# Key parts moved out a unit sooner, half of the sums split around the scores, slots and gates of one batch in one set of products

## The chip, the cores and the metric

The kernel runs on one core of a Trainium2 chip. A core has five engines that run side by side, each through its own instructions in order: TensorE (PE in the profile; PEld are its weight loads), VectorE (DVE), ScalarE (ACT), GpSimd (POOL) and SyncE (SP, which issues most DMAs here). They wait for one another through semaphores. The metric is the time of one execution in microseconds (us); lower is better.

## What is computed

Three stages in a row, float32 at the interface except for the weights of the second:

```python
# 1. bucketed attention: B=2, H=8, S=768, D=64, 6 projection bits
q_bucket = bits((q @ proj) > 0); k_bucket = bits((k @ proj) > 0)
scores = where(q_bucket == k_bucket, q @ k.T / 8, -1e9)
attn = softmax(scores)
x = (attn @ v) reshaped to 1536 x 512
# 2. gated layer, d_ff = 1536
y = ((x @ w_a) * (x @ w_b)) @ w_out
# 3. eight experts, d_ff = 1024: each token goes to the expert whose embedding is nearest
expert = argmax(cosine(y, emb) / tau); gate = softmax(...)[expert]
out[token] = gate * (relu(y @ w1[expert]) @ w2[expert])
```

The weights of stage 2 arrive as 64-bit floats and are converted on the chip; products that need more precision than one pass gives are made from a high and a low part of each operand.

## The kernel before

**Order.** The program runs under a manual schedule: what the Python code issues first on an engine runs first on that engine. Two places write that order out.

**Attention** (`attention`, lines 62 to 358) runs over 48 units `u` of 256 queries each: a pair of heads `i` has six units (`r = u % 6`), a head three (`s = u % 3`). A unit has two tiles `t`. For each, TensorE makes scores (`scores`, L205 and L208) in one of two PSUM tiles `st`; VectorE takes the row maximum (`rowmax`, L213); ScalarE the exponential with its sum (`expo`, L219), which frees the PSUM tile; GpSimd normalizes (`normal`, L228 to L232); two units later VectorE transposes the tile (`turn`, L239); and TensorE multiplies by the values (`pv`, L248, "the sums"), 24 blocks a head, in two PSUM tiles `pvb` of two banks each. The sums of a head run 12 blocks at the end of a unit with `s = 0` and 12 at the end of the next. In the unit with `s = 2` ScalarE copies the sums out (`epilogue`, L268), first one `pvb` tile, then the other.

The same two `pvb` tiles then serve the preparation of a later pair. Which one depends on the unit: the last unit of a pair transposes the keys and queries of a pair to come (`turned`, L114, L128), the third makes the sign bits of the next pair (`signs`, L154 to L181). Keys use `pvb[1]`, queries `pvb[0]`. The key part is issued on TensorE as soon as the first `epilogue` has freed its tile (`fresh`), the query part at the end of the unit. Each returns a function that moves the result out of PSUM. These functions are held in `preps` and called in the next unit, after its first exponential. The key signs go to a tile `sk` and to the list `later`; `masks()` (L143), called in each unit right ahead of `preps`, makes the two masked copies `kf` from `sk`.

Other work hangs on hooks in the units: `plan` lists, for conversions of the first weights (`split64`: the steps rest, top, low, add, size, guard, parts on VectorE, GpSimd and ScalarE), the unit of each of the seven steps.

**The rest** is a list `main` of named steps, with `after` and `chain` hanging side jobs behind them: `chain` puts one job behind each following step. `("p", c, t, f, w, h)` is half a product of the gated layer (six matmuls), `("o", c, t, m)` an output product, `("h", ...)`, `("t", ...)`, `("e", ...)` are hidden rows, their transposes and output products of the first expert. The routing of each of the two batches `b` runs between these: `route_choose` finds the expert (VectorE, L712 to L726), `route_places` each token's place (TensorE L734, L740; VectorE L747 to L755, which ends in six selection tiles `sel`), `route_slots` multiplies `sel` with token numbers (L771) to get the list of tokens that `gather` fetches, `route_gates` makes the gates (VectorE L789 to L799 with an exponential on ScalarE between), `route_gate_slots` multiplies the same `sel` with the gates (L806). `transpose_in` (L851) turns gathered rows. All of them draw on two PSUM tiles of the tag `rt` in turn.

Of the kernel before, what the change touches and what calls it, by code (L numbers as in the profile page):

```python
# [9 lines left out]
F32R = mybir.dt.float32r  # L10
# [15 lines left out]
class Kernel:  # L26
# [37 lines left out]
    def attention(self, xh, xl, pools, hook):  # L64
        nc = self.nc
# [249 lines left out]
        for u in range(NU + 2):  # L315
# [10 lines left out]
            if act:  # L326
                rowmax(u, 0)
                scores(u, 1)
            moves = [((u - 8) // 3, g) for g in (1, 0)] if s == 2 and u >= 8 else []
            for m in moves[:2 if u == NU - 1 else 1]:  # L330
# [27 lines left out]
            if new < len(pairs):  # L358
                preps, held, held_kind = fresh + [kind(new, x) for x in (1, 0)[len(fresh):]], new, kind
            elif s < 2 and u >= 6:  # L360
                pv((u - 6) // 3, range(12 * s, 12 * s + 12))
            hook(u, 0)
# [52 lines left out]
class Experts:  # L415
# [312 lines left out]
    def route_places(self, b):  # L728
# [20 lines left out]

        tl = self.tl = self.small("tl", [128, TB, 2, E], F32R)  # L750
        nc.vector.tensor_tensor(tl[:, :, 0], f32(oh), self.wide(self.tok), ALU.mult)
# [14 lines left out]
    def route_slots(self, b):  # L766
        nc = self.nc
        TB, E = self.TB, self.E
        q = self.rt.tile([128, 512], F32, tag="rt", name="slots")
        for t in range(TB):  # L770
            nc.tensor.matmul(  # L771
                q[:, :2 * E], self.sel[b, t], self.tl[:, t].rearrange("p a e -> p (a e)"),
                start=(t == 0), stop=(t == TB - 1),
            )
        gi = self.gi[b] = self.small("gi", [128, E], I32)
        nc.vector.tensor_copy(gi, q[:, :E])

        big = 4096.0
        oi = self.small("oif", [128, E])
        nc.vector.tensor_scalar(oi, q[:, E:2 * E], -big, big + b * self.S, ALU.mult, ALU.add)  # L780
        nc.vector.tensor_tensor(oi, oi, q[:, :E], ALU.add)
        so = self.so[b] = self.small("so", [128, E], I32)
        nc.vector.tensor_copy(so, oi)

    def route_gates(self, b):
# [10 lines left out]
        nc.vector.tensor_tensor(tg, f32(self.oh[b]), self.wide(gt), ALU.mult)  # L796
        th = self.th = self.small("th", [128, TB, 2, E], F32R)
        nc.vector.tensor_copy(th[:, :, 0], tg)
        nc.vector.tensor_tensor(th[:, :, 1], tg, f32(th[:, :, 0]), ALU.subtract)  # L799

    def route_gate_slots(self, b):
# [3 lines left out]
        for t in range(TB):  # L805
            nc.tensor.matmul(  # L806
                q[:, :2 * E], self.sel.pop((b, t)), self.th[:, t].rearrange("p a e -> p (a e)"),
                start=(t == 0), stop=(t == TB - 1),
            )
        sg = self.sg[b] = self.small("sg", [128, E])  # L810
        nc.vector.tensor_copy(sg, q[:, :E])
# [231 lines left out]
def tile_kernel(ctx, tc, q, k, v, proj, w_a, w_b, w_out, emb, tau, w1, w2, out, dbg=None):  # L1043
# [5 lines left out]
    with tc.manual_schedule():  # L1049
# [15 lines left out]
        with tc.tile_pool(name="conv", bufs=1, side="left") as X.conv, \  # L1065
# [7 lines left out]
            def late():  # L1073
# [8 lines left out]
                (3, 4, 5, 6, 6, 9, 12), (7, 10, 11, 12, 12, 13, 18), (15, 17, 19, 22, 22, 23, 28), (21, 25, 26, 28, 28, 29, 34),  # L1082
                (42, 43, 43, 44, 44, 44, 45),
            )
# [130 lines left out]
        after(("o", L, 2, 2), split, 0, 6, G)  # L1215
        after(("o", L, 3, 2), split, 0, 7, G)
        after(("e", 0, 1, 0), X.transpose_in, 1, 0)
        after(("e", 0, 1, 1), X.transpose_in, 1, 1)
# [10 lines left out]
        def begin():  # L1229
# [9 lines left out]
            (T, 3), (T, 4), [(T, 5), (X.route_norm, 0)], (GL, 1), [(GT, 1), (X.route_choose, 0)],  # L1239
            None, None, None, (X.route_places, 0), None, [(X.route_slots, 0), (X.gather, 0, 0)],  # L1240
            (X.route_gates, 0), None, None, None, None, None, (X.route_gate_slots, 0),
        ])
        chain(("o", L, 2, 1), [(T, 6), (T, 7), (T, 8), (GL, 2), (GT, 2)])
        after(("p", L, 3, 1, 1, 1), begin)
        after(("o", L, 3, 0), X.transpose_in, 0, 0)
        after(("o", L, 3, 0), X.gather, 1, 0)
# [7 lines left out]
        after(("e", 0, 0, 2), X.gather, 1, 1)  # L1254
        after(("e", 0, 1, 0), X.route_gate_slots, 1)
        after(("h", 1, 0), X.route_most)
# [46 lines left out]
```

## Time and profile before

| | |
|---|---|
| median of 3 runs | 738.56 us (737.71 to 740.46) |
| the profiled execution | 737.05 us, of which the profile spans 735.3 us |
| TensorE busy over the span | 702.2 us (96%) |
| VectorE, GpSimd, ScalarE busy | 463.3, 440.6, 353.4 us |
| granted TensorE clock, mean | 0.997 |

The profile shows one execution. Busy time is the time in which an engine had an instruction running; "idle before" a row is the time its engine stood before it, with what ended the wait. Neighbours on one engine overlap a little, so a row's length and the distance to the next row's start differ.

### The profile page before, as it was taken

The numbers are of one execution on the slowest core, as the hardware profiler recorded it, in microseconds if no ns is written. First come the engines' busy times: TensorE is split into PE (matmuls) and PEld (weight loads), VectorE is DVE, ScalarE is ACT, GpSimd is POOL, SyncE is SP. The second block draws the span as 40 slices with busy tenths as digits, with TensorE's granted clock in tenths as the row PEclk, the third lists the DMA queues.
The fourth block names the chain that finished last, engine by engine and source line by source line (L and its number), as shares of the span: only waits on it lengthen the run. The fifth ranks groups of instructions, "written<-read, shape, count | busy, mean of one in ns | idle before, by whom it ended". The sixth has DMA issues, their size and how long they took to land.

```text
span 735.3 us, 16440 instructions
## 1 busy us (share of the span) xinstructions
PE 702.2 (96%) x6793; PEld 582.2 (79%) x6793; DVE 463.3 (63%) x675; ACT 353.4 (48%) x651; POOL 440.6 (60%) x453
## 2 busy tenths in 40 slices
PE   6799998999989999999999999999999999999996
PEld 4355554555658999999999999998888999889995
DVE  3999989888885554645646546534744865555650
ACT  4677877787664333212121212234436655556551
POOL 1777998988785572653645636634513866556651
PEclk9999999999999999999999999999999999999998
DMA  6955567364233230220211211354251966566510
GB/s 160 182 127 138 115 144 162 84 130 118 46 90 119 81 116 1 91 83 23 93 58 58 63 53 58 121 162 148 70 175 33 297 240 204 212 223 244 204 56 23
DMA packets 68605, 88.31 MB, mean 120 GB/s; under 512 B 28963, under 2 KB 41123, under 8 KB 68528
## 3 DMA queue, kind: packets, MB, share of 16 engines
q1 hardware_dynamic: 64320, 79.49, 37.5%
q0 software_dynamic: 2560, 7.34, 2.6%
q8 instruction: 54, 0.88, 0.5%
q10 hardware_dynamic: 1648, 0.39, 0.3%
q14 instruction: 23, 0.19, 0.1%
HBM read 75.52 MB, written 7.34 MB: 113 GB/s over the span
## 4 chain that ended last, share of the span: by engine, by line
PE 78%; DVE 7%; ACT 4%; issue 4%; DMA 4%; POOL 2%; SPq 1%; POOLq 0%; DVEq 0%; ACTq 0%
PE ab L548 24%; PE yp L580 13%; PE op L924 10%; PE hp L874 10%; PE pv L248 8%; PE st L205 5%; DVE nm L213 3%; ACT e L219 2%; DVE et L239 2%; PE part L548 2%; PE hr L892 2%; DMA vr<-in_v_dram 1%; PE xgt L851 1%; PE st L208 1%; DMA raw<-in_k_dram 1%
## 5 line engine op out<-in xcount | busy, mean ns | idle before, releaser
L548 PE MATMUL ab<-xh,w 128*128 128x384 f32 x704 | 185.7, 338 | 0.0
L548 PEld LDWEIGHTS ab<-xh,w 128*128 128x128 f32 x704 | 127.7, 188 | 2.0 <-issue 1.2
L548 PE MATMUL ab<-xl,w 128*128 128x384 f32 x352 | 118.3, 336 | 0.0
L563 POOL TENSOR_TENSOR g<-a,g 128x384 fp32r<-128x384 f32 x48 | 53.9, 1123 | 106.1 <-ACT g L562 106.1
L830 POOL TENSOR_TENSOR w<-raw,w 128x1024 fp32r<-128x1024 f32 x36 | 88.1, 2448 | 35.7 <-ACT w L829 34.6
L219 ACT ACTIVATE e<-st,nm 128x768 f32<-128x768 f32 x96 | 86.6, 903 | 41.1 <-DVE nm L213 19.9
L580 PE MATMUL yp<-w,g 128*128 128x512 f32 x432 | 102.9, 390 | 0.0
L213 DVE TENSOR_REDUCE nm<-st 128x1 f32<-128x768 f32 x96 | 90.2, 940 | 19.3 <-PE st L208 19.0
L232 POOL TENSOR_SCALAR e<-e,s,mc 128x768 f32<-128x768 f32 x96 | 95.2, 999 | 5.4 <-POOL s L230 0.2
L239 DVE STREAM_TRANSPOSE et<-e 128x768 f32<-128x768 f32 x96 | 92.3, 963 | 3.3 <-issue 1.3
L205 PE MATMUL st<-ks,qs 64*128 64x384 f32 x192 | 85.6, 526 | 8.9 <-ACT e L219 8.2
L205 PE MATMUL st<-k,q 64*128 64x384 f32 x192 | 85.8, 527 | 8.0 <-ACT e L219 7.0
L580 PEld LDWEIGHTS yp<-w,g 128*128 128x128 f32 x432 | 80.4, 188 | 14.9
L924 PE MATMUL op<-w,hth 128*128 128x512 f32 x256 | 80.8, 396 | 0.0
L874 PE MATMUL hp<-xgh,w 128*128 128x256 f32 x448 | 80.7, 281 | 0.0
L562 ACT CAST g<-a 128x384 fp32r<-128x384 f32 x48 | 24.7, 515 | 105.1 <-DVE a L561 105.1
L248 PEld LDWEIGHTS pv<-et,vr 32*64 32x64 f32 x3072 | 59.6, 130 | 19.3 <-issue 9.3
L248 PE MATMUL pv<-et,vr 32*64 32x192 f32 x3072 | 71.1, 325 | 3.8 <-ACT q L128 1.9
L830 DVE TENSOR_TENSOR w<-raw,w 128x1024 fp32r<-128x1024 f32 x28 | 64.9, 2316 | 14.4 <-ACT w L829 14.2
L874 PEld LDWEIGHTS hp<-xgh,w 128*128 128x128 f32 x448 | 69.1, 188 | 0.3
L548 PEld LDWEIGHTS ab<-xl,w 128*128 128x128 f32 x352 | 66.2, 188 | 0.8
L557 ACT COPY a<-ab 128x384 f32<-128x384 f32 x44 | 21.0, 478 | 94.6 <-PE ab L548 93.2
(202 smaller groups left out, 1242.2 us busy)
## 6 DMA issues: line engine op xcount, KB each, us to landing
raw<-in_moe_w_dram SPq DMA_DIRECT2D x32, 1024.0 KB, 5.2
vr<-in_v_dram SPq DMA_DIRECT2D x64, 192.0 KB, 4.2
raw<-in_moe_w_a_dram SPq DMA_DIRECT2D x5, 1024.0 KB, 5.2
raw<-in_moe_w_b_dram SPq DMA_DIRECT2D x5, 1024.0 KB, 5.1
raw<-in_moe_w_out_dram SPq DMA_DIRECT2D x5, 1024.0 KB, 5.0
raw<-in_k_dram SPq DMA_DIRECT2D x16, 192.0 KB, 4.9
qs<-q SPq DMA_DIRECT2D x16, 192.0 KB, 4.0
ybuf<-y SPq DMA_DIRECT2D x12, 256.0 KB, 6.0
```

What stands on the lines that cost most here:

```text
L205: nc.tensor.matmul(st[:, n, :H2], q[d, ql], k[d], start=True, stop=False, tile_position=(64 * n, 0))
L213: nc.vector.tensor_reduce(NM[u][:, t:t + 1], ST[u, t][:, :, :H2], axis=AX.XY, op=ALU.max, negate=True)
L219: nc.scalar.activation(e, ST.pop((u, t))[:, :, :H2], AF.Exp, bias=NM[u][:, t:t + 1], accum_out=SU[u][:, t:t + 1])
L232: nc.gpsimd.tensor_scalar(E[u, t], E[u, t], r[:, t:t + 1], c[:, t:t + 1], ALU.mult, ALU.add)
L239: nc.vector.transpose(ET[h][:, :, c], E.pop((u, t)).rearrange("p a (b s) -> p (a b) s", s=32))
L248: nc.tensor.matmul(pvb[a // 2][m:m + 64, a % 2, :NC * 32], v[d], et[d, n].rearrange("p c s -> p (c s)"), start=(n < 2), stop=(n >= NB32 - ...
L548: nc.tensor.matmul(p[:, :384], w[:, k, fs], x[:, k, cols], start=(k == 0 and n == 0), stop=(k == self.KD - 1 and n == 2),)
L563: nc.gpsimd.tensor_tensor(gl[:, f], a, f32(gh[:, f]), ALU.subtract)
L580: nc.tensor.matmul(p, g[:, f, rows], w[:, f], start=(n == 0), stop=(n == 5))
L830: eng.tensor_tensor(l, raw, f32(h), ALU.subtract)
L874: nc.tensor.matmul(p[:, :256], w[:, k, fs], x[:, k], start=(n == 0), stop=(n == 3 * self.KD - 1))
L924: nc.tensor.matmul(p, h[:, 2 * n + f, rows], w[:, f], start=(n == 0 and f == 0 and m == 0), stop=(n == 3 and f == 1 and m == 2),)
```

## The change

The function that moves a key part out is called in the unit that issued it, after that unit's second exponential; the query part stays held for the next unit. Of the first twelve blocks of a head's sums, six stay at the end of the unit with `s = 0`, and six go into the next unit between its two scores. In the plan of the first weights' last piece, `guard` and `parts` move one unit later. For the first batch, gates are computed before places, and slots and gates come from one set of products with 32 columns; its places, slots and transpose move one step later in the list. For the second batch, the gate products come before the transpose that follows the same step.

```diff
@@ -326,6 +326,8 @@
             if act:
                 rowmax(u, 0)
                 scores(u, 1)
+            if s == 1 and u >= 7:
+                pv((u - 7) // 3, range(6, 12))
             moves = [((u - 8) // 3, g) for g in (1, 0)] if s == 2 and u >= 8 else []
             for m in moves[:2 if u == NU - 1 else 1]:
                 epilogue(*m)
@@ -356,9 +358,11 @@
             if act:
                 expo(u, 1)
             if new < len(pairs):
-                preps, held, held_kind = fresh + [kind(new, x) for x in (1, 0)[len(fresh):]], new, kind
+                for prep in fresh:
+                    prep(nc.scalar)
+                preps, held, held_kind = [kind(new, x) for x in (1, 0)[len(fresh):]], new, kind
             elif s < 2 and u >= 6:
-                pv((u - 6) // 3, range(12 * s, 12 * s + 12))
+                pv((u - 6) // 3, range(12, NB32) if s else range(6))
             hook(u, 0)
             if s == 1 and u >= 7 and (u - 1) // 3 < 2 * len(pairs):
                 load_v((u - 1) // 3)
@@ -747,7 +751,10 @@
         nc.vector.tensor_tensor(tmp, p[:, :TB * E].rearrange("p (t e) -> p t e", e=E), f32(oh), ALU.mult)
         nc.vector.tensor_reduce(pos, tmp, axis=AX.X, op=ALU.add)
 
-        tl = self.tl = self.small("tl", [128, TB, 2, E], F32R)
+        if b:
+            tl = self.tl = self.small("tl", [128, TB, 2, E], F32R, bufs=1)
+        else:
+            tl = self.tl
         nc.vector.tensor_tensor(tl[:, :, 0], f32(oh), self.wide(self.tok), ALU.mult)
         nc.vector.tensor_copy(tl[:, :, 1], oh)
         for t in range(TB):
@@ -767,9 +774,10 @@
         nc = self.nc
         TB, E = self.TB, self.E
         q = self.rt.tile([128, 512], F32, tag="rt", name="slots")
+        n = 2 if b else 4
         for t in range(TB):
             nc.tensor.matmul(
-                q[:, :2 * E], self.sel[b, t], self.tl[:, t].rearrange("p a e -> p (a e)"),
+                q[:, :n * E], self.sel[b, t] if b else self.sel.pop((b, t)), self.tl[:, t].rearrange("p a e -> p (a e)"),
                 start=(t == 0), stop=(t == TB - 1),
             )
         gi = self.gi[b] = self.small("gi", [128, E], I32)
@@ -781,6 +789,8 @@
         nc.vector.tensor_tensor(oi, oi, q[:, :E], ALU.add)
         so = self.so[b] = self.small("so", [128, E], I32)
         nc.vector.tensor_copy(so, oi)
+        if b == 0:
+            self.slot_gates(b, q[:, 2 * E:])
 
     def route_gates(self, b):
         nc = self.nc
@@ -794,7 +804,11 @@
         nc.vector.reciprocal(gt, gt)
         tg = self.small("tg", [128, TB, E])
         nc.vector.tensor_tensor(tg, f32(self.oh[b]), self.wide(gt), ALU.mult)
-        th = self.th = self.small("th", [128, TB, 2, E], F32R)
+        if b:
+            th = self.th = self.small("th", [128, TB, 2, E], F32R, bufs=1)
+        else:
+            self.tl = self.small("tl4", [128, TB, 4, E], F32R, bufs=1)
+            th = self.tl[:, :, 2:]
         nc.vector.tensor_copy(th[:, :, 0], tg)
         nc.vector.tensor_tensor(th[:, :, 1], tg, f32(th[:, :, 0]), ALU.subtract)
 
@@ -807,6 +821,10 @@
                 q[:, :2 * E], self.sel.pop((b, t)), self.th[:, t].rearrange("p a e -> p (a e)"),
                 start=(t == 0), stop=(t == TB - 1),
             )
+        self.slot_gates(b, q)
+
+    def slot_gates(self, b, q):
+        nc, E = self.nc, self.E
         sg = self.sg[b] = self.small("sg", [128, E])
         nc.vector.tensor_copy(sg, q[:, :E])
         nc.vector.tensor_tensor(sg, q[:, E:2 * E], sg, ALU.add)
@@ -1080,7 +1098,7 @@
             plan = {(-1, 0): [jobs[0][0], jobs[1][0]], (37, 1): [outs[0][0]], (47, 1): [outs[1][0]]}
             places = (
                 (3, 4, 5, 6, 6, 9, 12), (7, 10, 11, 12, 12, 13, 18), (15, 17, 19, 22, 22, 23, 28), (21, 25, 26, 28, 28, 29, 34),
-                (42, 43, 43, 44, 44, 44, 45),
+                (42, 43, 43, 44, 44, 45, 46),
             )
             plan[NU + 2, 3] = outs[1][1][:4]
             plan[NU + 2, 4] = outs[1][1][4:6]
@@ -1214,6 +1232,7 @@
         after(("o", L, 2, 1), split, 0, 5, G)
         after(("o", L, 2, 2), split, 0, 6, G)
         after(("o", L, 3, 2), split, 0, 7, G)
+        after(("e", 0, 1, 0), X.route_gate_slots, 1)
         after(("e", 0, 1, 0), X.transpose_in, 1, 0)
         after(("e", 0, 1, 1), X.transpose_in, 1, 1)
         for n, at in enumerate((("t", 0, 1, 1), ("e", 0, 1, 1), ("e", 0, 1, 2), ("e", 0, 1, 3))):
@@ -1237,12 +1256,11 @@
         chain(("o", L, 0, 2), [(T, 0), (T, 1), (T, 2), (GL, 0), (GT, 0)], 2)
         chain(("o", L, 1, 2), [
             (T, 3), (T, 4), [(T, 5), (X.route_norm, 0)], (GL, 1), [(GT, 1), (X.route_choose, 0)],
-            None, None, None, (X.route_places, 0), None, [(X.route_slots, 0), (X.gather, 0, 0)],
-            (X.route_gates, 0), None, None, None, None, None, (X.route_gate_slots, 0),
+            None, None, (X.route_gates, 0), None, (X.route_places, 0), None, [(X.route_slots, 0), (X.gather, 0, 0)],
         ])
         chain(("o", L, 2, 1), [(T, 6), (T, 7), (T, 8), (GL, 2), (GT, 2)])
         after(("p", L, 3, 1, 1, 1), begin)
-        after(("o", L, 3, 0), X.transpose_in, 0, 0)
+        after(("o", L, 3, 1), X.transpose_in, 0, 0)
         after(("o", L, 3, 0), X.gather, 1, 0)
         chain(("o", L, 3, 1), [
             (T, 9), [(T, 10), (R, 9)], [(T, 11), (X.route_norm, 1), (R, 10)], [(R, 11), (X.route_choose, 1)],
@@ -1252,7 +1270,6 @@
         after(("h", 0, 1, 0), X.route_gates, 1)
         after(("e", 0, 0, "half"), X.transpose_in, 0, 1)
         after(("e", 0, 0, 2), X.gather, 1, 1)
-        after(("e", 0, 1, 0), X.route_gate_slots, 1)
         after(("h", 1, 0), X.route_most)
         for e in range(2, X.E):
             for b in range(B):
```

## Rows read from the trace of the kernel before

**Rows 1.** windows by stage: stretch, length, busy us of each engine (instructions), clock, DMA

```profile
36.00:187.00 151.00, 141.60 (x2835) 82.66 (x2832) 135.52 (x190) 116.48 (x238) 125.25 (x213) 1.00 0.54 124
...
236.00:505.00 269.00, 269.00 (x1440) 252.15 (x1439) 140.28 (x191) 72.06 (x132) 141.48 (x83) 1.00 0.23 79
505.00:562.00 57.00, 55.02 (x378) 49.04 (x377) 32.37 (x100) 24.00 (x46) 19.70 (x13) 1.00 0.36 115
562.00:720.00 158.00, 158.00 (x1044) 144.19 (x1045) 95.09 (x101) 91.32 (x139) 99.53 (x53) 1.00 0.56 196
```

**Rows 2.** waits of TensorE, 36 to 216 us: total, times, longest

```profile
PE st L205 <- ACT e L219: 8.5, 21, 1.1
```

**Rows 3.** timeline, unit after a transposed pair: start, length, instruction, [idle before]

```profile
114.22 0.90 ACT L219 ACTIVATE e<-st,nm 128x768 f32<-128x768 f32 x1 [0.65 <-DVE r L223]
...
115.12 0.80 ACT L128 ACTIVATE k<-pv 128x768 f32<-128x768 f32 x1
...
115.27 0.59 PE L205 MATMUL st<-k,q 64*128 64x384 f32 x1 [0.57 <-ACT e L219]
...
115.81 0.81 ACT L128 ACTIVATE q<-pv 128x768 f32<-128x768 f32 x1
...
116.67 2.21 PE L248 MATMUL pv<-et,vr 32*64 32x192 f32 x96 [0.32 <-ACT q L128]
```

**Rows 4.** timeline, unit after sign bits

```profile
49.35 0.90 ACT L219 ACTIVATE e<-st,nm 128x768 f32<-128x768 f32 x1 [0.36 <-DVE r L223]
...
50.24 0.57 ACT L154 ACTIVATE sk<-pv,bias 128x384 bf16<-128x384 f32 x1
...
50.39 0.59 PE L205 MATMUL st<-ks,qs 64*128 64x384 f32 x1 [0.28 <-ACT e L219]
...
50.70 0.58 ACT L154 ACTIVATE qf<-pv,bias 128x384 bf16<-128x384 f32 x1
...
51.40 2.21 PE L248 MATMUL pv<-et,vr 32*64 32x192 f32 x96
...
54.43 1.11 ACT L143 ACTIVATE kf<-sk,fac 128x384 bf16<-128x384 bf16 x2
```

**Rows 5.** timeline, two units with conversions on ScalarE

```profile
38.88 2.21 PE L248 MATMUL pv<-et,vr 32*64 32x192 f32 x96 [0.32 <-ACT q L128]
...
39.28 0.90 ACT L219 ACTIVATE e<-st,nm 128x768 f32<-128x768 f32 x1
...
62.17 0.90 ACT L219 ACTIVATE e<-st,nm 128x768 f32<-128x768 f32 x1 [0.28 <-DVE r L223]
...
64.62 2.21 PE L248 MATMUL pv<-et,vr 32*64 32x192 f32 x96 [0.32 <-ACT q L128]
...
65.53 0.92 ACT L219 ACTIVATE e<-st,nm 128x768 f32<-128x768 f32 x1
```

**Rows 6.** timeline, the guard of the first weights' last piece

```profile
205.40 1.22 DVE L473 SCALAR_TENSOR_TENSOR late<-late 128x512 f32<-128x512 f32 x1 [1.09 <-POOL late L462]
```

**Rows 7.** timeline, routing of the first batch, and one line's instructions in both

```profile
513.62 2.40 POOL L830 TENSOR_TENSOR w<-raw,w 128x1024 fp32r<-128x1024 f32 x1
...
516.62 0.20 PE L734 MATMUL pos<-ohb,tri 128*128 128x56 bf16 x1 [0.76 <-DVE ohb L724]
...
518.81 1.19 PEld L771 LDWEIGHTS slots<-tl,sel 128*128 128x128 f32 x6
...
520.71 0.20 DVE L789 TENSOR_TENSOR lg<-lg,mx 128x48 f32<-128x48 f32 x1
...
522.62 0.55 DVE L561 TENSOR_TENSOR a<-ab,a 128x384 f32<-128x384 f32 x1
...
530.52 0.86 PEld L806 LDWEIGHTS gates<-th,sel 128*128 128x128 f32 x6
...
L718 DVE TENSOR_TENSOR eq<-eq,em x2: 210/1266/2321, 513.8 to 542.2; 128x48 f32<-128x48 f32 x2
```

**Rows 8.** timeline, routing of the second batch

```profile
561.88 0.66 PE L907 MATMUL ht<-ident,hs 128*128 128x128 f32 x4 [0.89 <-DVE xgl L855]
```

## Prediction

> **What bounds the kernel now.** I read the windows by stage first [rows 1]. From 36 to 187 us (attention) TensorE is busy 141.6 of 151 us, from 236 to 505 us and from 562 to 720 us it is busy all the time, and in the routing stretch from 505 to 562 us it is busy 55.0 of 57. So TensorE sets the pace everywhere; what the change can win is TensorE's idle time in two stretches, some 9 us and 2 us, and whatever it wins or loses there reaches the end undiminished, since nothing behind has slack. The waits of TensorE come next [rows 2]: in attention it waits mostly in front of scores, for the exponential that frees their PSUM tile, 21 times and 8.5 us. Then the timeline, for the three kinds of unit that the change touches [rows 3 to 6], and for the routing of the first and the second batch [rows 7, 8].
>
> **Key parts one unit sooner, pair being transposed (five times).** Now ScalarE runs the exponential, the key copy and the query copy in a row, and the sums start after the query copy [rows 3]: 114.22, 115.12, 115.81, sums at 116.67, which is 1.40 after the scores' start at 115.27. With the key copy gone ahead, the query copy starts at 115.12 and ends at 115.93; then the scores in front bind, 1.01 us for a scores block that starts after a wait (50.39 to 51.40 in a like unit, which ScalarE no longer holds back), so sums at 116.28: 0.39 sooner. The key copy now stands in the idle time ahead of the exponential. In a row it costs 0.69 (115.12 to 115.81); the idle time is 0.65 here and, at its least, 0.28 [rows 3, 5], plus the 0.1 by which neighbours overlap. So it is hidden in the one and delays by 0.3 in the other, which leaves 0.39 and 0.07. The others lie between: 0.2 each, five times, -1.0 us. Its two swap DMAs are issued on SyncE a unit sooner, with nothing queued that another waits for: nothing.
>
> **Key parts one unit sooner, signs (six times).** Here the step drags another along. The sign of the key appends to a list, and the list is worked off by `masks()`, which stands ahead of the held parts in the next unit. Today the key sign and the query sign run in one unit and the two mask products (1.11 us the pair, 1.01 net of the overlap) a unit later, where no sums wait [rows 4]. After the change the key sign hides (0.46 net, in idle time of 0.36 plus the overlap), but the mask products come between the exponential and the query sign. What began at 50.24 with the key sign begins with the masks: 50.24 + 1.01 + 0.58 for the query sign + 0.05 to release = 51.88, where the sums started at 51.40. They write the bank that the query sign reads, and the next scores stand behind them on TensorE: +0.48, six times, +2.9 us. The bounds: 0 if the sums were not held, 1.01 if the whole mask time were exposed.
>
> **Twelve blocks split into six and six.** The work is the same; what changes is what waits. With six blocks (half of twelve, which take 2.21, some 2.14 of it before the next scores can start) after the held parts, the second scores of the next unit come 1.07 us sooner and can meet an exponential that is not done. In the seventh unit the sums start at 38.88, six blocks end at 39.95, and the exponential that frees the tile starts at 39.28 and lets scores start 1.05 later (114.22 to 115.27 in [rows 3]), 40.33: +0.4. In the unit around 63 us [rows 5] the first exponential starts at 62.17, the query copy 1.59 behind it as in [rows 3], at 63.76, and the second exponential at 65.53. After the change the first starts 0.3 later, the query copy 0.90 behind it, at 63.37, the second exponential 1.77 behind that as now, at 65.14, and scores at 66.19, against sums that start at 64.62 - 0.07 = 64.55 and six blocks that end at 65.62: +0.6. Two long conversions of the first weights on ScalarE make it so; the other units have none. On the other side the second six blocks fill waits in front of scores, between none and all of the 8.5 us. Most of these waits follow directly on other scores with no sums in reach, so I take 0.6.
>
> **The weights' guard and parts one unit later.** VectorE stands 1.09 us for GpSimd's add and then needs 1.22 [rows 6]. Moved, the wait goes, but the operation returns one unit on, ahead of another row maximum, on an engine busy 135.5 of 151 us. Between 0 and -1.1, I take -0.2.
>
> **Slots and gates of the first batch together.** Removed: six weight loads and six narrow products, 0.86 us [rows 7]. Places stand one half product later, which removes the wait of 0.76 before them. But the gates' VectorE work, 1.91 us from 520.71 to 522.62, now stands between the choice and the places, and the six `sel` tiles behind it. The last would come 1.91 later, while slots have only one half product more in front of them; two take from 516.82 to 518.81, so one takes 1.0. From the same point of the program, +1.91 - 1.0 = +0.9 (the removed wait of 0.76 is in this, since the chain on VectorE, not TensorE, decides): TensorE stands some 1.9 us ahead of slots. Wider products (32 columns for 16) cost nothing, the loads set their pace. The gather starts 1.9 later and its transpose one output product later; it had 8 us. The sum of this part is about 0, between -0.8 and +0.9.
>
> The 1.91 is a span with GpSimd idle. In the choice just ahead, one small product of VectorE took 2.32 us in the first batch and 0.21 in the second; the long one began 0.15 after a 2.40 us weight subtraction of GpSimd and ended with it [rows 7]. The Trainium skill ("SBUF — State Buffer", Who interferes with whom) says why: a VectorE operation with two SBUF inputs and a GpSimd operation that reads SBUF share a port as an exclusive lock, and whoever starts second waits for the whole of the other. The trace agrees. By the row of the gates this part comes to about 0; by the rule, if such a subtraction began first, to +2.4.
>
> **Gates of the second batch before the transpose.** The transposes of the hidden rows wait 0.89 us for a tile that VectorE empties last [rows 8]. With the order turned, that tile is the gates', emptied by two short copies before the other transposes end: -0.9 us.
>
> **The sum.** -1.0 + 2.9 + 0.4 + 0.6 - 0.6 - 0.2 + 0.9 - 0.86 - 0.9 = +1.2 us. The profiled execution took 737.05, so 738.3; the median of the runs is 1.5 above it: 739.8.
>
> **Rivals.**
> *Attention does not react* (0.2): sums and scores shift against each other, and VectorE, busy 135.5 of 151 us, sets the units as before. Against it: TensorE, not VectorE, has the fewest gaps. Only routing and guard remain, 0.9 - 0.86 - 0.9 - 0.2 = -1.1: 737.5.
> *The split fills the waits* (0.08), the other side: all 8.5 us in front of scores go instead of 0.6, 7.9 less: 731.9. It decides (3.7 us below) from 5.5 of the 8.5 on. For it: the six blocks stand just in front of such scores. Against it: the waits lie mostly in units without sums.
> *ScalarE becomes the bound* (0.12): the mask time is exposed whole, 1.01 for 0.48, +3.2, and nothing is filled, +0.6: 743.6. For it: exponentials of the same unit stand behind masks and signs. Against: six blocks lie between them and the scores that need them. It passes the bound of slower from 0.9 a unit on.
> *A lock in the gates* (0.1): one product of the choice took 2.32 us beside a weight subtraction of 2.40 [rows 7]; if one of the gates' four two-input products, now ahead of the places, meets such a subtraction, slots wait 2.4 more: 742.2. Against it: the weight split before ends at 516.02, ahead of the gates' start at some 516.8, and the next stands seven steps of the order behind them. The lock rule named above would make it so only if the subtraction started first.
>
> **Numbers.** The forecast has 0.5. A measurement of this kernel can tell some 0.5% (3.7 us) from no change. Faster: the filling rival and a little, 0.09. Slower: the ScalarE rival and the edge of the lock, 0.16. Within: 0.75. The range goes from 736.2 (masks not exposed, -2.9, and the first batch's part at its low bound, -0.7) to 742.8 (mask time exposed almost whole, +3.0); it leaves out the filling rival and most of the ScalarE one.
>
> **What would show it.** Mask products between exponential and query sign, and sums 1.5 us after the scores' start in six units (now 1.0); in five others 1.0 after it (now 1.4). New waits in front of scores around 40 and 66 us. A stall of about 2 us before slots, none before places, no second set of gate products for the first batch, and no wait before the hidden transposes of the second. The prediction is wrong if sums do not wait for the query sign, or if the routing chain on VectorE is not as serial as I take it.

## The result, and the profile after

The changed kernel took 746.59 us (median of 6 runs, 744.52 to 748.82) where the kernel before, beside it, took 738.83 (6 runs, 737.71 to 740.46): ratio 1.0105, 95% interval [1.0088, 1.0122], 7.8 us slower. The forecast was 739.8 us, its range ended at 742.8. The profiled execution of after took 746.42 us, its span 744.6.

The windows by stage of after, with the stretches of [rows 1]:

```profile
36.00:187.00 151.00, 140.38 (x2640) 77.89 (x2640) 131.98 (x183) 112.44 (x232) 121.56 (x206) 1.00 0.52 123
...
505.00:562.00 57.00, 54.32 (x340) 47.03 (x337) 30.99 (x92) 22.21 (x45) 21.26 (x13) 0.97 0.37 115
562.00:720.00 158.00, 157.96 (x1044) 143.70 (x1044) 92.81 (x104) 91.89 (x139) 97.78 (x54) 1.00 0.61 199
```

In attention TensorE is as busy as before (140.4 of 151 us against 141.6), and every other engine is less busy in the same stretch: all of it runs later, and TensorE fills the time with something. In the routing stretch the granted clock is 0.97 where it was 1.00.

The waits of TensorE from 36 to 216 us in after, beside [rows 2] (total, times, longest):

```profile
PE st L205 <- ACT e L219: 8.2, 22, 1.1
PE pv L248 <- ACT qf L154: 2.4, 6, 0.4
```

The second line is new: six waits of 0.4 us, sums behind the query sign. This makes 2.4 us; the waits in front of scores are much the same. So most of what attention lost is no wait.

To find it I set the start of each unit's first exponential in after against its start in before. The delay grows from 0.16 us in the sixth unit to 6.45 in the last, stands at 7.13 all through the stretch of full load, goes to 9.23 in the routing of the first batch, to 10.19 and back to 9.37 in the second, and stays. Attention and routing therefore lost 6.3 and 2.2 us; 0.7 came between them, at one "issue" gap that grew from 0.80 to 1.48. The delay also grows there in the kernels with one part alone that are described below (split 0.66, key parts 0.68, routing 0.34), and the gap is 1.21 in a kernel that is unchanged up to there (the last edit alone, below). So at least a part of it comes without the change; I have no cause for it.

Where attention lost it shows in one head's sums. The timeline of TensorE in before, behind the sums of [rows 3]:

```profile
118.81 0.59 PE L205 MATMUL st<-k,q 64*128 64x384 f32 x1
...
119.56 0.32 PE L208 MATMUL st<-kf,qg 64*128 64x384 bf16 x1
...
119.72 0.48 PE L205 MATMUL st<-k,q 64*128 64x384 f32 x1
...
120.37 0.32 PE L208 MATMUL st<-kf,qg 64*128 64x384 bf16 x1
...
120.63 2.21 PE L248 MATMUL pv<-et,vr 32*64 32x192 f32 x96
122.76 0.59 PE L205 MATMUL st<-k,q 64*128 64x384 f32 x1
```

And the timeline of the same stretch in after, with ScalarE's copies ahead of it:

```profile
117.58 0.80 ACT L128 ACTIVATE k<-pv 128x768 f32<-128x768 f32 x1
118.28 0.90 ACT L219 ACTIVATE e<-st,nm 128x768 f32<-128x768 f32 x1
...
119.15 0.82 ACT L128 ACTIVATE q<-pv 128x768 f32<-128x768 f32 x1
...
119.32 0.59 PE L205 MATMUL st<-k,q 64*128 64x384 f32 x1 [0.50 <-ACT e L219]
...
120.33 1.23 PE L248 MATMUL pv<-et,vr 32*64 32x192 f32 x48
121.49 0.59 PE L205 MATMUL st<-k,q 64*128 64x384 f32 x1
...
122.50 1.23 PE L248 MATMUL pv<-et,vr 32*64 32x192 f32 x48
123.66 0.59 PE L205 MATMUL st<-k,q 64*128 64x384 f32 x1
...
124.67 2.21 PE L248 MATMUL pv<-et,vr 32*64 32x192 f32 x96
126.80 0.59 PE L205 MATMUL st<-k,q 64*128 64x384 f32 x1
```

Read start to start, no line here has an idle time in front of it but the first scores. Before: twelve blocks 2.14 (116.67 to 118.81), scores 0.91, scores 0.91, twelve blocks 2.13: 6.09. After: six blocks 1.16, scores 1.01, six blocks 1.16, scores 1.01, twelve blocks 2.13: 6.47. The same products take 0.38 us more: half of twelve would be 1.07, but six blocks take 1.16 (+0.09, twice), and scores with sums on both sides take 1.01 where scores behind scores or in front of scores took 0.91 (+0.10, twice). Scores that start behind a wait also take 1.01 up to sums (119.32 to 120.33), so a change of shape costs the scores behind it what a start behind a wait does. Fourteen heads have scores between the two halves: 14 x 0.38 = 5.3 us. The groups on the page of the profile show it as idle time of the weight loads of the sums that nothing in the profile ends ("issue"): 16.6 us in after; before it was 9.3. In the timeline of before, the weight load of scores behind scores starts 0.16 us ahead of its product (119.56 for 119.72), but that of sums behind scores starts only with the product (120.63).

```profile
L248 PEld LDWEIGHTS pv<-et,vr 32*64 32x64 f32 x3072 | 58.4, 130 | 27.4 <-issue 16.6
```

```profile
119.56 0.19 PEld L205 LDWEIGHTS st<-k,q 64*128 64x128 f32 x1 [0.22 <-issue]
...
120.63 1.86 PEld L248 LDWEIGHTS pv<-et,vr 32*64 32x64 f32 x96 [0.48 <-issue]
```

The unit after sign bits in after, beside [rows 4], is as forecast: masks between exponential and query sign, and sums 1.47 behind the scores' start (132.23 to 133.70; forecast 1.5, before 1.0). In the unit above, after a transposed pair, the key copy is gone ahead and the sums start 1.01 behind the scores (119.32 to 120.33; before 1.40).

```profile
132.07 1.11 ACT L143 ACTIVATE kf<-sk,fac 128x384 bf16<-128x384 bf16 x2
...
132.23 0.59 PE L205 MATMUL st<-ks,qs 64*128 64x384 f32 x1 [0.28 <-ACT e L219]
...
133.08 0.57 ACT L154 ACTIVATE qf<-pv,bias 128x384 bf16<-128x384 f32 x1
...
133.70 1.24 PE L248 MATMUL pv<-et,vr 32*64 32x192 f32 x48 [0.40 <-ACT qf L154]
```

The routing in before, where [rows 7, 8] don't show it (timeline):

```profile
522.12 2.89 PE L580 MATMUL yp<-w,g 128*128 128x512 f32 x12
...
528.93 0.60 PE L851 MATMUL xgt<-ident,xg 128*128 128x128 f32 x4
...
531.40 0.85 PE L681 MATMUL lgt<-yt,enT 128*32 128x384 f32 x8
```

The routing of after (timeline, and two windows of 3 us):

```profile
527.08 0.25 PE L779 MATMUL slots<-tl,sel 128*128 128x32 f32 x1 [0.68 <-DVE sel L762]
527.93 1.06 PE L779 MATMUL slots<-tl,sel 128*128 128x32 f32 x5 [0.59 <-DVE sel L762]
...
530.15 4.33 PE L584 MATMUL yp<-w,g 128*128 128x512 f32 x12
...
539.89 0.85 PE L685 MATMUL lgt<-yt,enT 128*32 128x384 f32 x8
...
561.13 0.63 PE L869 MATMUL xgt<-ident,xg 128*128 128x128 f32 x4 [1.16 <-DMA xg<-ybuf,gi]
...
529.00:532.00 3.00, 3.00 (x11) 2.63 (x12) 1.39 (x7) 0.95 (x2) 1.55 (x2) 0.62 0.17 35
532.00:535.00 3.00, 3.00 (x15) 2.41 (x14) 1.18 (x2) 1.83 (x4) 3.00 (x2) 0.81 0.13 52
```

The forecast stall in front of slots is there (0.68 and 0.59; the delay grows from 7.13 to 8.03, +0.9). Behind it the granted clock is 0.62 and 0.81, that is, TensorE ran partly at its lower level of 1.2 GHz, and twelve products took 4.33 us, where before they took 2.89 (522.12 above): +1.44. Then two edits overlap. The transpose of the first batch's gathered rows is gone from its old place (528.93 in before), -0.43, and stands further back (540.67), where it costs 0.73. The removed gate products give 0.55 back: the delay is 9.04 ahead of them and 8.49 at the products behind them (531.40 to 539.89). The three make -0.25. The second batch's transpose meets a new wait of 1.16 for the gathered rows, +0.97, and the turned order behind it gives 0.82.

### The profile page after: what moved, and what is told of

Its sections match the earlier page's. It is cut to its first block, busy times and chain, and to the rows that moved or that the text cites. A ratio compares the mean times of both kernels' runs of the same rounds, so it can differ in the third digit from the quotient of the medians.

```text
span 744.6 us, 16429 instructions
## 1 busy us (share of the span) xinstructions
PE 708.3 (95%) x6787; PEld 580.7 (78%) x6787; DVE 462.8 (62%) x675; ACT 352.4 (47%) x651; POOL 442.4 (59%) x453
## 4 chain that ended last, share of the span: by engine, by line
PE 77%; DMA 7%; ACT 6%; issue 4%; DVE 3%; SPq 2%; POOL 0%; POOLq 0%; ACTq 0%; DVEq 0%
PE ab L552 24%; PE yp L584 13%; PE op L942 10%; PE hp L892 10%; PE pv L248 9%; PE st L205 5%; ACT e L219 3%; DMA vr<-in_v_dram 3%; PE part L552 2%; DVE nm L213 1%; DMA spare<-in_moe_w_b_dram 1%; PE st L208 1%; DMA ybuf<-y 1%; PE xgt L869 1%; PE hr L910 1%
## 5 line engine op out<-in xcount | busy, mean ns | idle before, releaser
L584 PE MATMUL yp<-w,g 128*128 128x512 f32 x432 | 104.4, 394 | 0.0
L248 PEld LDWEIGHTS pv<-et,vr 32*64 32x64 f32 x3072 | 58.4, 130 | 27.4 <-issue 16.6
L248 PE MATMUL pv<-et,vr 32*64 32x192 f32 x3072 | 74.7, 327 | 5.2 <-ACT qf L154 2.4
L566 ACT CAST g<-a 128x384 fp32r<-128x384 f32 x48 | 24.7, 515 | 107.1 <-DVE a L565 107.1
L589 DVE TENSOR_TENSOR y<-yp,y 128x512 f32<-128x512 f32 x60 | 41.5, 692 | 40.5 <-PE yp L584 40.5
```

What stands on the lines that cost most here:

```text
L248: nc.tensor.matmul(pvb[a // 2][m:m + 64, a % 2, :NC * 32], v[d], et[d, n].rearrange("p c s -> p (c s)"), start=(n < 2), stop=(n >= NB32 - ...
L584: nc.tensor.matmul(p, g[:, f, rows], w[:, f], start=(n == 0), stop=(n == 5))
```

## The experiments

Theory: a cut of the sums by scores costs TensorE 0.38 us, whatever it meets there; the key parts lose by the masks and gain by the copies; in the routing, TensorE's wait costs more than its length, because the clock falls behind it. Rivals: the split loses to late exponentials; VectorE sets the units' pace; the routing loses its time in the gates on VectorE. Each ratio is to the kernel before on the same chip. In some of the profiles (among them the split alone, the slots later, and the gates earlier) the clock also fell to the lower level once or twice between 20 and 44 us, where the kernels do much the same and TensorE waits 1.2 us several times; so in those delays are read from the twelfth unit on or over one head.

**The parts alone.** The split alone is the first hunk of the diff and the two ranges; the keys alone is its hunk on `preps`; the routing alone is the hunks from `route_places` on, the guard left out; the fourth is the changed kernel with the split undone:

```diff
-            if s == 1 and u >= 7:
-                pv((u - 7) // 3, range(6, 12))
...
-                pv((u - 6) // 3, range(12, NB32) if s else range(6))
+                pv((u - 6) // 3, range(12 * s, 12 * s + 12))
```

> The kernel before with the split of the first twelve blocks alone. Theory 1, switches: the split adds a change from sums to scores and one from scores to sums in each head, and TensorE pays 0.38 us for the two together (in the trace of after, two times six blocks and two scores take 4.34 us where twelve blocks and two scores took 3.96), so 14 heads cost 5.3 us, and with the waits of 0.4 and 0.6 near 40 and 66 us about 6 us: ratio 1.008. Theory 2, waits only: the split costs the two waits, 1.0 us, and wins back up to 0.6: ratio 1.000 to 1.001.

> The kernel before with key parts moved out a unit sooner alone. Theory 1: the mask products ahead of the query sign cost 0.48 us in six units, the transposed pairs win 0.2 in five, so +1.9 us: ratio 1.0025. Theory 2, the step is the main loss: the six half periods that hold the signs grew by 3.9 us in the changed kernel, all of it by this step, +3 to +4 us: ratio 1.004 to 1.005. A third, that sums hide it: 1.000.

> The kernel before with the routing part of the change alone (slots and gates together for the first batch, gates before the transpose for the second). Theory 1: the stall before slots costs what was forecast, and TensorE's clock falls to half for 3.4 us behind it again (+1.4 to +1.7), so -0.9 + 1.5 = +0.6, and up to 1.0 more where the second batch's gather waits for the store of its rows: ratio 1.000 to 1.002. Theory 2, the fall of the clock has nothing to do with this part: -0.9 us, ratio 0.999, and a granted clock of 1.00 throughout the routing.

> The changed kernel with the twelve blocks back in one piece. Theory 1, switches: 5 to 6 us less than the changed kernel, about 741 us: ratio 1.003. Theory 2, waits only: 1 us less, about 745.5 us: ratio 1.009.

Measured: split alone 744.04 us, 1.0067 [1.0040, 1.0093]; keys alone 739.99, 1.0016 [0.9999, 1.0033]; routing alone 740.98, 1.0032 [1.0009, 1.0054]; all but the split 741.86, 1.0045 [1.0026, 1.0064]. The split is the largest part. It loses although its waits in front of scores fell, from 8.5 us to 7.7, its two new ones (0.17 and 0.72) included. The keys alone show the six waits of 0.4 us for the query sign again, and their delay grows by 1.5 us in attention (sign units +2.3, turned units -0.8). The routing alone repeats the stall (+1.1), the lower clock behind it (+1.2) and the late gather (+1.7), and -0.8 from the turned order. Between keys alone and all but the split, the guard's move makes no difference: the delay grows by 1.26 from the twelfth to the last unit in the one and by 1.28 in the other. The profile of the latter shows the guard's 2.1 us gone in one unit and back in the next.

**The cut elsewhere.** The first twelve in one piece, the second twelve cut by scores:

```diff
+            if s == 1 and u >= 7:
+                pv((u - 7) // 3, range(12, 18))
...
-                pv((u - 6) // 3, range(12 * s, 12 * s + 12))
+                pv((u - 6) // 3, range(18, NB32) if s else range(12))
```

> The kernel before with the second twelve blocks split instead of the first (six between the scores of that unit, six at its end). No held part and no conversion stands ahead of these blocks, so no exponential is late for them. Theory 1, switches: the same two additional changes in each of 14 heads, 5.3 us, ratio 1.007. Theory 2, the loss of the split is its place, that is, exponentials that are not done: 0 to 0.5 us, ratio 1.000.

Measured: 742.14 us, 1.0043 [1.0029, 1.0058]. A cut of the other half, with other neighbours, costs about as much: one head's stretch, from the first of its sums to the scores behind the last, takes 6.47 us (121.42 to 127.89 in its timeline), as in after, where before took 6.09. In all it cost 3.3 us and not the 5.3 expected; a part of the difference is that it fills waits too (7.4 us in front of scores, where before had 8.5).

**No cut at all.** All 24 blocks of a head in one piece:

```diff
-            elif s < 2 and u >= 6:
-                pv((u - 6) // 3, range(12 * s, 12 * s + 12))
+            elif s == 0 and u >= 6:
+                pv((u - 6) // 3, range(NB32))
```

> The kernel before with all 24 blocks of a head in one piece at the end of the unit that had the first twelve. Theory 1 alone: one pair of changes fewer in each of 14 heads, -5.3 us, ratio 0.993. Against it: one piece holds TensorE for 4.3 us, in which the other engines have scores for two tiles only (some 3 us of VectorE's work), so that VectorE stands and the next units are bound by it: same or up to +10 us, ratio 1.000 to 1.013.

Measured: 766.75 us, 1.0377 [1.0327, 1.0426]. Its waits in front of scores are 24.7 us (29 times): in a piece of over 4 us ScalarE and VectorE run out of scores. What the saved cut gives shows all the same, in the timeline:

```profile
71.64 4.16 PE L248 MATMUL pv<-et,vr 32*64 32x192 f32 x192 [0.32 <-ACT q L128]
75.73 0.59 PE L205 MATMUL st<-k,q 64*128 64x384 f32 x1
```

Up to the next scores, 24 blocks in one piece take 4.09 us where nothing interrupts them; two pieces of twelve take 2 x 2.14 = 4.28. Pieces of 6, 12 and 24 blocks (1.16, 2.14, 4.09) lie on one line: 0.163 us a block and 0.19 for each piece, however long. The sums have to be cut somewhere; the length of a piece is bounded from both sides.

**A change of shape with nothing moved.** The weights of a score product take 64 rows and 128 columns of TensorE, those of a sum 32 and 64 (the 64\*128 and 32\*64 of the rows above). One product of one column was set into the middle of the second twelve, in the scores' shape, and as a control in the sums' own. Its result goes to a column that nothing reads.

```diff
-                pv((u - 6) // 3, range(12 * s, 12 * s + 12))
+                if s == 1 and act:
+                    pv((u - 6) // 3, range(12, 18))
+                    nc.tensor.matmul(
+                        pvb[0][:, 1, 448:449], QF[i][:64, :128], KF[i][:64, 0, :1], start=False, stop=False, tile_position=(0, 0)
+                    )
+                    pv((u - 6) // 3, range(18, NB32))
...
```

> The kernel before with one product more in each of fourteen heads: in the middle of the second twelve blocks stands a product of one column whose weights take 64 rows and 128 columns of TensorE, as those of the scores do, where the products of the blocks take 32 rows and 64 columns. It goes to a column of PSUM that nothing reads; nothing else is changed, no work is moved and no engine waits for it. Theory: what the split costs is TensorE's change from the one shape to the other and back, 0.38 us for the two; then each such product costs some 0.4 us, fourteen of them 5.3 us, ratio 1.007, and the second six blocks start some 0.3 us or more behind the first six. Rival: the split costs by what stands beside it, scores that come sooner against exponentials and VectorE; then one narrow product costs its own length, under 0.1 us, fourteen of them under 1.4 us, ratio 1.000 to 1.002.

> The control of the run before: the same single product at the same place, with weights of 32 rows and 64 columns, as the blocks' own. Both theories: its own length alone, under 0.05 us, fourteen of them under 0.7 us, ratio 1.000 to 1.001. If it costs as much as the foreign one, the cost lies in any further product there and not in the change of shape.

Measured: foreign 740.79 us, 1.0031 [1.0014, 1.0047]; like 738.99, 0.9992 [0.9978, 1.0006]. The foreign product cost 2.0 us, less than I expected and more than the rival did, but the interval reaches down to the rival's 1.002. So here the timeline decides. With the foreign product:

```profile
122.32 1.23 PE L248 MATMUL pv<-et,vr 32*64 32x192 f32 x48
123.48 0.17 PE L363 MATMUL pv<-kf,qf 64*128 64x1 bf16 x1
123.59 1.23 PE L248 MATMUL pv<-et,vr 32*64 32x192 f32 x48
124.75 0.59 PE L205 MATMUL st<-k,q 64*128 64x384 f32 x1
```

With the like one:

```profile
122.62 1.35 PE L248 MATMUL pv<-et,vr 32*64 32x192 f32 x49
123.65 0.16 PE L364 MATMUL pv<-et,vr 32*64 32x1 f32 x1
...
124.83 0.59 PE L205 MATMUL st<-k,q 64*128 64x384 f32 x1
```

The twelve blocks and the foreign product take 2.43 us (122.32 to 124.75), with the like one 2.21, without either 2.13. Six blocks between two other shapes take 1.16 (122.32 to 123.48 and 123.59 to 124.75), as the six blocks in after do, and nothing was moved here and nothing waits. So the blocks' half of the 0.38 belongs to the change of shape on TensorE, in the middle of running work: a narrow product costs 0.30 in the foreign shape and 0.08 in the blocks' own. Fourteen times 0.30 would be 4.2 us; the delay grew by 3.2 from the seventh unit to the last (0.12 to 3.31); of the other 1.0, 0.5 shows as shorter waits in front of scores (8.0 for 8.5). The foreign product differs from the blocks in its type as well, bf16 for f32. The rows of before speak against that as the cause: f32 scores start 0.16 behind bf16 ones of the same shape (119.56 to 119.72), sums 0.26 behind them (120.37 to 120.63), so the change of type goes without the 0.10 that the change of shape takes. The Trainium skill ("TensorEngine Tiling (Array Packing)", Key Properties) says that a change of the tiling mode, unlike one of the tile, drains TensorE. These runs agree: each change takes about 0.1 us from the blocks beside it. That rule speaks against the split, and my prediction did not weigh it.

**Masks out of the way.** The keys alone, but masks only in a unit without held parts, where they ran before:

```diff
-            masks()
+            if not preps:
+                masks()
...
-                preps, held, held_kind = fresh + [kind(new, x) for x in (1, 0)[len(fresh):]], new, kind
+                for prep in fresh:
+                    prep(nc.scalar)
+                preps, held, held_kind = [kind(new, x) for x in (1, 0)[len(fresh):]], new, kind
```

> Key parts a unit sooner, but the mask products left where they were (masks are skipped in a unit that has held parts). Theory 1: the loss of the six sign units goes, the win of the transposed pairs stays: -0.8 to -1.0 us, ratio 0.999, against +1.5 with the masks ahead. Theory 2, moving key parts is a loss by itself: still +1 to +2 us, ratio 1.002.

Measured: 737.41 us, 0.9976 [0.9963, 0.9990]. The waits for the query sign are gone, attention gains 0.9 us (the delay goes from 0.12 in the sixth unit to -0.82 in the last). The loss in the sign units is the masks, and without them the early key parts gain.

**Slots later.** The routing alone, with slots and the first gather two steps later:

```diff
-            None, None, (X.route_gates, 0), None, (X.route_places, 0), None, [(X.route_slots, 0), (X.gather, 0, 0)],
+            None, None, (X.route_gates, 0), None, (X.route_places, 0), None, None, None, [(X.route_slots, 0), (X.gather, 0, 0)],
```

> The routing part alone, with slots and gather two steps later in the list, so that the selection tiles are there when TensorE comes to them. Theory 1, the stall makes the clock fall: no stall, a granted clock of 1.00 from 505 to 562 us, and over the routing -0.9 - 0.9 - 0.8 = -2.5 us, or -1.5 if the second gather still waits 1.0 for the store; ratio 0.997 to 0.998. Theory 2, the clock falls for another reason of the new order (narrow products, fewer loads): 0.97 again, +0.5 us.

Measured: 738.35 us, 0.9991 [0.9970, 1.0012]. The wait in front of slots is gone, and with it the lower clock there: up to 545 us the clock is 1.00. But the second batch's transpose now waits longer for its rows, and the clock falls behind that wait. The time lies between the two theories, and the clock over the whole stretch is 0.97 as the second had it:

```profile
553.48 0.63 PE L865 MATMUL xgt<-ident,xg 128*128 128x128 f32 x4 [2.30 <-DMA xg<-ybuf,gi]
...
505.00:545.00 40.00, 39.75 (x273) 35.13 (x273) 26.74 (x74) 19.45 (x39) 17.09 (x10) 1.00 0.46 144
545.00:562.00 17.00, 14.70 (x89) 13.06 (x88) 5.07 (x25) 5.17 (x8) 2.94 (x3) 0.90 0.19 61
```

The lower clock left its place with the one wait and came behind another. That is no rule for any wait: the one of 1.16 us in after (561.13) has a clock of 1.00 behind it. Why the gather is late in the kernels with the routing change is open: GpSimd waits for the store of the second batch's rows, which lands later against TensorE's work than before.

**What gained, together.** Keys with masks later; places of the first batch one step later, gates on their own and behind slots; gates of the second batch ahead of the transpose. And that last edit alone:

```diff
-            None, None, None, (X.route_places, 0), None, [(X.route_slots, 0), (X.gather, 0, 0)],
-            (X.route_gates, 0), None, None, None, None, None, (X.route_gate_slots, 0),
+            None, None, None, None, (X.route_places, 0), None, [(X.route_slots, 0), (X.gather, 0, 0)],
+            (X.route_gates, 0), None, None, None, None, (X.route_gate_slots, 0),
...
+        after(("e", 0, 1, 0), X.route_gate_slots, 1)
         after(("e", 0, 1, 0), X.transpose_in, 1, 0)
...
-        after(("e", 0, 1, 0), X.route_gate_slots, 1)
```

> The kernel before with what the runs so far showed to gain: key parts one unit sooner, but the mask products left out of a unit with held parts, so that they run a unit later; places of the first batch one step later, its slots, gather and gates where they were and gates still on their own behind slots; gates of the second batch before the transpose. Theory: each part brings what it brought alone, since no new wait of TensorE of 1 to 2 us arises and so no stretch at half clock: keys about 0.9 us (attention gained 0.8 to 0.9 in the run with masks later), the removed wait before places at most 0.76, the turned order in the second batch 0.8; 2.5 us in all, ratio about 0.9965. Rival: the places a step later only move the wait to slots, as they did with the gates in front; then TensorE waits there, the clock falls to its half level once more, and 1.7 of the 2.5 us are lost, ratio about 0.999.

> The kernel before with one edit alone: gate products of the second batch ahead of the transpose of its rows. Theory: the wait of 0.89 us ahead of the hidden transposes goes, the tile that they need being emptied by two short copies: 0.8 us, ratio about 0.999. Rival: the wait belongs to the gathered rows or to GpSimd and stays, or moves to the gate products: 0.0, ratio 1.000.

Measured: the last edit alone 737.87 us, 0.9981 [0.9968, 0.9994]; its delay falls by 0.82 at the second batch's hidden transposes, which wait no longer. The parts together 742.11, 1.0038 [1.0027, 1.0050]: slower, by neither theory. The timeline of their routing, and a window:

```profile
522.05 1.28 ACT L793 ACT_TABLE_LOAD   x1
...
523.62 0.20 DVE L795 TENSOR_REDUCE gt<-lg 128x6 f32<-128x48 f32 x1 [2.02 <-ACT lg L793]
...
524.60 2.34 POOL L833 TENSOR_TENSOR w<-raw,w 128x1024 fp32r<-128x1024 f32 x1 [1.47 <-ACT w L832]
...
524.75 2.25 DVE L802 TENSOR_TENSOR th<-tg,th 128x48 fp32r<-128x48 f32 x1
526.92 1.28 DVE L588 TENSOR_TENSOR y<-yp,y 128x512 f32<-128x512 f32 x2
...
527.66 1.12 PE L656 MATMUL yt<-ident,y 128*128 128x128 f32 x4 [4.12 <-DVE y L588]
...
526.00:529.00 3.00, 1.34 (x6) 1.25 (x6) 2.39 (x4) 1.36 (x3) 0.94 (x1) 0.66 0.20 30
```

The gates had slipped a step with slots, and two things followed. VectorE stood 2.02 us for the gates' exponential (0.40 in the kernel before), whose table load of 1.28 us on ScalarE now came behind a cast of that step. Then the gates' last product began 0.15 behind a weight subtraction of GpSimd and ended with it, 2.25 us where it takes 0.21. `y` stood behind both on VectorE, and TensorE waited 4.12 us, again with a low clock behind. By these rows the long product made some 2.0 of the 4.12 (2.25 - 0.21), an estimate, and the order of the work the rest. The long product is the lock of my fourth rival, in another kernel than I feared it for. The Trainium skill ("SBUF — State Buffer", Who interferes with whom) says that a VectorE operation with two SBUF inputs and a GpSimd operation that reads SBUF exclude each other; these two rows agree. In the next run the gates go back into the step of slots, which takes them away from the subtraction and from that cast at once and can't tell the two parts from each other:

```diff
-            None, None, None, None, (X.route_places, 0), None, [(X.route_slots, 0), (X.gather, 0, 0)],
-            (X.route_gates, 0), None, None, None, None, (X.route_gate_slots, 0),
+            None, None, None, None, (X.route_places, 0), None, [(X.route_slots, 0), (X.gather, 0, 0), (X.route_gates, 0)],
+            None, None, None, None, None, (X.route_gate_slots, 0),
```

> The run of the good parts with one edit: the gates' VectorE work of the first batch in the step of slots instead of one step behind it, so that it stands ahead of the next unit's addition, as in the kernel before. Theory: what made that run slow was the last of the four two-input products of the gates, 2.25 us (0.21 in the kernel before), which began 0.15 after a 2.34 us weight subtraction of GpSimd and ended with it; the y behind it on VectorE came late, TensorE stood 4.12 us ahead of its transpose and ran at the half level after it. One step earlier the product ends by some 522.2 us, before the subtraction begins at 524.6: no product over 0.3 us, no wait over 1 us in the routing of the first batch, clock 1.00 there; the gains of the parts stay, -0.9 in attention, -1.0 at places, -0.8 in the second batch, 2.7 us in all, ratio about 0.9963. Rival: places and slots a step later are themselves what delays y; then the wait ahead of the transpose stays above 1 us and the ratio is 1.000 or more.

Measured: 736.70 us, 0.9964 [0.9950, 0.9978], the lowest ratio of this study, 2.1 us (0.4%) under the kernel before. The same product, 0.21 us, now ends 2.1 us ahead of the subtraction, and the clock of the routing is 1.00:

```profile
525.63 0.21 DVE L802 TENSOR_TENSOR th<-tg,th 128x48 fp32r<-128x48 f32 x1
...
527.92 4.76 POOL L833 TENSOR_TENSOR w<-raw,w 128x1024 fp32r<-128x1024 f32 x2
...
505.00:562.00 57.00, 56.65 (x382) 50.27 (x381) 33.00 (x99) 25.44 (x48) 20.87 (x14) 1.00 0.38 120
```

From the twelfth unit on its delay falls by 0.8 in attention (3.54 to 2.72), by 1.0 at places (3.14 to 2.10), by 0.8 at the second gates (2.19 to 1.37): the 2.7 expected.

## Why the prediction was wrong

The forecast was +1.2 us, the profile shows +9.3 in the span. The step that failed is "Twelve blocks split into six and six. The work is the same; what changes is what waits." It is not the same on TensorE: 14 x 0.38 = 5.3 us that the sum held at zero. The row of the sums already showed a part of the price: I halved 2.14, the length of twelve blocks up to the next scores, as if none of it were the change of shape, where 0.19 of it are.

By the terms of the sum:

- **Turned pairs, -1.0.** Right in mechanism, -0.8 with the keys alone.
- **Signs, +2.9.** Right in mechanism and nearly in size: +2.3 with the keys alone, and gone with the masks moved.
- **New waits of the split, +0.4 and +0.6.** Both there in after, 0.22 and 0.43.
- **Filled waits, -0.6.** The split alone lowers the waits in front of scores by 0.8 net of its two new ones, so it fills some 1.7 (0.8 + 0.17 + 0.72). The filling rival had a part of the truth, and the changes of shape outweighed it: from the twelfth unit on, where twelve of the fourteen cuts lie, 12 x 0.38 - 0.8 = 3.8, and the delay of the split alone grew there by 3.7 (3.14 to 6.85).
- **Guard, -0.2.** 0.0.
- **Slots stall, +0.9.** Measured +0.9, on VectorE's chain as worked out. What it cost further was missing: +1.4 by the lower clock behind the wait. [rows 1] showed the routing at 1.00, and the step took a wait as worth its own length. That the wait causes the lower clock is argued from its place in four kernels (after, the routing alone and all but the split have both, slots later has neither there); why other waits left the clock at 1.00 stays open.
- **Gate products, -0.86.** -0.55. I took the length of their weight loads; they overlap with the work around them.
- **Turned order in the second batch, -0.9.** -0.8.
- **Not in the sum:** the first batch's transpose at its later place, +0.3; the late gather of the second batch, +1.0, its cause open; 0.7 between attention and the full stretch, cause open.

Of the rivals, attention did react and ScalarE became no bound: its exposed mask time was what the sum had. The lock did not occur in the changed kernel, whose gates ran between two subtractions, but it did one step of the order away.

## What to carry to other kernels

Where products of different tile shapes alternate on a full TensorE, count the changes of shape: here a cut with two more changes cost 0.38 us without a single wait in the trace, more than the waits that it filled. Look at what follows a wait of TensorE as well as at its length, since twelve products behind two short waits took half as long again, though not every wait did this. An operation of VectorE with two inputs moved by one step can land beside a long one of GpSimd, and one that needs ScalarE behind other work there; look at what both do at the new place before moving it.

## What the hardware showed unexpectedly

- Some waits of TensorE in the routing were followed by a lower granted clock in windows of 3 to 17 us, wherever they stood: two waits of 0.68 and 0.59 us close together by 0.62 and 0.81 (after), one of 4.12 by 0.66 (the good parts), one of 2.30 by 0.90 (slots later); in two more kernels with the pair of waits (the routing alone, all but the split) the routing stretch had 0.97. Others left it at 1.00: 0.76 and 0.89 us in the kernel before, 1.16 in after, 1.86 in the routing alone (the last two for gathered rows). So did most waits of 1.1 us in attention. I can't say from these runs what tells them apart.
- Start to start, score products of 0.91 us took 1.01 when sums stood on both sides, and six blocks took 1.16 for 1.07, in rows of the products that show no idle time; a piece of sums between scores costs 0.19 us beyond its blocks, whether it has 6, 12 or 24.
